# Rounding g and subtracting its high part on two pairs of chunks at once, and without plain f32 pairs

## The chip, the core and the metric

The kernel runs on one core of a Trainium2 chip. A core has TensorE (PE; PEld is its weight load), VectorE (DVE), ScalarE (ACT), GpSimd (POOL) and SyncE (SP, which issues the DMAs here). The metric is the device time of one execution, in microseconds.

## The reference

Four batches of 12480 tokens, 128 channels, 49 agents, all float32. An attention through agents is followed by a layer with 2048 hidden units:

```python
a2k = softmax(scale * agents @ k.T)      # per batch, 49 x 12480
agent_v = a2k @ v                        # 49 x 128
q2a = softmax(scale * q @ agents.T)      # 12480 x 49
x = q2a @ agent_v                        # all batches: 49920 x 128
h = x @ w_in                             # 49920 x 2048
g = h - np.tanh(h)
out = g @ w_out                          # 49920 x 128
```

## The kernel before

**Precision.** A matmul on f32 operands is replaced by several on float32r (fp32r) operands: a value is rounded to fp32r (its high part), and the difference is a second fp32r value (its low part). `w_out` is kept as `wo_h` and `wo_l`, and a hidden activation g as `gh` and `gl`. Then g @ w_out is gh x wo_l + gh x wo_h + gl x wo_h: three matmuls in place of one.

**First stage** (lines 482 to 502). For batch 0 the keys' scores, their maximum, the weighted values and the decoding of the 64-bit weights run by themselves, up to about 86 us. `agent_v` of a batch is multiplied into `w_in` (`project`), which gives `aw`, 98 x 2048: 49 rows for the high part and 49 for the low part of the softmax of q.

**Main stage** (from line 503). The tokens of all batches are cut into 104 blocks of 480 (`BLK`), and the 2048 hidden units into 16 chunks of 128 (`NCH`). The unit of work is a pair of chunks, so that a block has 8 pairs (`HP`) and the whole 832. One pair goes through these steps:

- `m1` (393 to 400) on PE: four matmuls of 480 columns, L398 and L399, write h of the pair into two banks of PSUM. Three such tiles (`ph`) exist.
- `act` (405 to 413): ACT takes the tanh of h (L408, into y) and squares it (L410, into z); DVE multiplies h by z (L412), which gives g. For the small h here g is proportional to h times tanh squared; the factor comes at the end, in `finish`.
- `high` (440) on POOL rounds g to gh (L442).
- `low` (445) on DVE subtracts gh from g, which gives gl (L447).
- `m2` (450 to 461) on PE: six matmuls, L459 to L461, add the pair's part to a PSUM tile `acc` of the block (from the pool `misc` of two tiles, which all the side work uses too).

In every second block (`PLAIN_EVERY`) the last pair is a plain one: it has no high and low, and `m2` multiplies g in f32 with an f32 copy of the weights, `wo_f` (L457, two matmuls; the profile records each of them as two).

The loop (553 to 586) writes one pair a step: m1, the side work, act and high of pair i, then low of pair i - 1 (`LAG1`), then m2 of pair i - 2 (`LAG2`). The queues `q1` and `q2` hold what is under way. Behind a block's last m2 `finish` copies `acc` to `out` on ACT (L522), and SP stores it after every second block. The framework then orders each engine's instructions by a simulated timeline, so an engine's order isn't exactly that of the loop.

**Side work** is cut into generators that are advanced by one piece in a step: the q softmax for two blocks (349 to 379: scores L353 on PE, maxima, sums and a product on DVE, two subtractions on POOL at L366 and L378), its transposition (L385, L390), and for the next batch one job of keys, maximum, values or projection at three places of every 16 steps (`KS`; L228, L276, L264). In the last batch there is no next one to prepare.

**Buffers.** y and z have 2 tiles, g 4, gh 3, gl 2, all of 960 columns. Keys have 3 tiles of their own in the main stage, values 4 (`VB`), which carry one more column, of ones.

Of the kernel before, what the change touches and what calls it, by code (L numbers as in the profile page):

```python
# [11 lines left out]
F32 = mybir.dt.float32  # L12
# [14 lines left out]
NCH = FF // 128  # L27
# [45 lines left out]
class Build:  # L73
# [19 lines left out]
    def constants(self):  # L93
# [15 lines left out]
        self.wo_f = c.tile([128, 2, C], F32, tag="wo_f", name="wo_f")  # L109
        self.vb = [c.tile([128, GT, C + 2], F32, tag=f"v{i}", name=f"v{i}") for i in range(VB)]  # L110
        for vt in self.vb:
            nc.gpsimd.memset(vt[:, :, C : C + 1], 1.0)
# [38 lines left out]
    def load_w_out(self, c, raw):  # L151
# [7 lines left out]
        if c == PLAIN_PAIR // 2:  # L159
            nc.scalar.copy(self.wo_f.rearrange("p n e -> p (n e)"), w[:, 2 * C * (PLAIN_PAIR % 2) :][:, : 2 * C])  # L160

    def phase1(self, b):
        nc = self.nc
        st = {}
        kb, vb = (KV0 if b == 0 else KV), VB
# [29 lines left out]
        def scores(g):  # L195
# [62 lines left out]
        def av(g):  # L258
            vt = ahead("v", load_v, g, vb - 1)
# [142 lines left out]
    def pair(self, t):  # L402
        return t[:, : 2 * BLK].rearrange("p (c n) -> p c n", c=2)

    def act(self, h):
        nc = self.nc
        y = self.pair(self.wtile("y", NB["y"]))
        nc.scalar.activation(y, h[:, :, :BLK], AF.Tanh, scale=TSC)  # L408
        z = self.wtile("z", NB["z"])[:, : 2 * BLK]
        nc.scalar.activation(z, y.rearrange("p c n -> p (c n)"), AF.Square)  # L410
        g = self.wtile("g", NB["g"])[:, : 2 * BLK]
        nc.vector.tensor_tensor(self.pair(g), h[:, :, :BLK], self.pair(z), ALU.mult)  # L412
        return g

    def act_general(self, h):
        nc = self.nc
        hv = h[:, :, :BLK]
        d = self.wtile("y", NB["y"])[:, : 2 * BLK]
        u = self.wtile("z", NB["z"])[:, : 2 * BLK]
        nc.scalar.activation(self.pair(d), hv, AF.Tanh)  # L420
        nc.scalar.activation(self.pair(u), hv, AF.Square)
        nc.vector.tensor_tensor(self.pair(d), hv, self.pair(d), ALU.subtract)
        big = self.wtile("y", NB["y"])[:, : 2 * BLK]
        nc.vector.tensor_scalar(big, u, 4.0, None, ALU.is_ge)
        nc.vector.tensor_scalar(u, u, 16.0, None, ALU.min)
        r = self.wtile("z", NB["z"])[:, : 2 * BLK]
        nc.vector.tensor_scalar(r, u, 1.0 / 15.0, 13.0, ALU.mult, ALU.add)
        g = self.wtile("g", NB["g"])[:, : 2 * BLK]
# [7 lines left out]
        nc.vector.tensor_tensor(self.pair(g), hv, self.pair(g), ALU.mult)  # L436
        nc.vector.copy_predicated(g, big.bitcast(I32), d)
        return g

    def high(self, g):  # L440
        gh = self.wtile("gh", NB["gh"])[:, : 2 * BLK].bitcast(F32R)
# [3 lines left out]
    def low(self, g, gh):  # L445
        gl = self.wtile("gl", NB["gl"])[:, : 2 * BLK].bitcast(F32R)
# [3 lines left out]
    def m2(self, acc, i, gh, gl):  # L450
        nc = self.nc
        for c in range(2):
            f = 2 * i + c
            x = slice(c * BLK, (c + 1) * BLK)
            first, last = f == 0, f == NCH - 1
            if gl is None:
                nc.tensor.matmul(acc[:, :BLK], self.wo_f[:, c, :], gh[:, x], start=first, stop=last)  # L457
                continue
            nc.tensor.matmul(acc[:, :BLK], self.wo_l[:, f, :], gh[:, x], start=first, stop=False)  # L459
            nc.tensor.matmul(acc[:, :BLK], self.wo_h[:, f, :], gh[:, x], start=False, stop=False)  # L460
            nc.tensor.matmul(acc[:, :BLK], self.wo_h[:, f, :], gl[:, x], start=False, stop=last)  # L461

    def fast(self):
        nc, tc = self.nc, self.tc
        HP = NCH // 2
        blocks = [(b, j) for b in range(B) for j in range(NBLK)]
        steps = [(n, i) for n in range(len(blocks)) for i in range(HP)]
# [64 lines left out]
        def rest(n, i, h):  # L532
            g = self.act(h)
            even = n % PLAIN_EVERY == 0
            plain = even and i == PLAIN_PAIR
            gh = None if plain else self.high(g)
            q1.append((n, i, g, gh))

        def low(keep):
            while len(q1) > keep:  # L540
                n, i, g, gh = q1.pop(0)
                q2.append((n, i, g, None) if gh is None else (n, i, gh, self.low(g, gh)))

        def out(keep):
            while len(q2) > keep:
# [3 lines left out]
                self.m2(acc[n], i, gh, gl)  # L549
                if i == HP - 1:  # L550
                    done.append(n)

        for n, i in steps:
            b = blocks[n][0]
            pos = (n % 2) * HP + i
# [3 lines left out]
            h = foreground(n, i)  # L559
            if n == 0 and i < len(rest0):  # L560
                run(rest0[i])
            nxt = []
            for gen in live:
                try:
                    next(gen)
                    nxt.append(gen)
                except StopIteration:
                    pass
            live[:] = nxt
            rest(n, i, h)  # L570
            low(LAG1)
            out(LAG2)
# [71 lines left out]
```

## Time and profile before

| | |
|---|---|
| runs, us | 2228.47, 2228.51, 2228.87 |
| median, us | 2228.51 |
| span of the profiled execution, us | 2226.8 |
| mean granted clock of TensorE | 0.992 |
| moved by DMA | 108.75 MB, 49 GB/s in the mean |
| batches 0 to 3 begin (first m1), us | 86.6, 634.7, 1180.7, 1726.5 |

The page gives no time of its own for the profiled execution beside its span; the three runs lie within 0.4 us of one another.

A busy time is the union of an engine's records. Matmuls are pipelined: a record of 0.38 us can stand behind one that started 0.22 us before, so the rate of PE is read from the distance of starts. "Idle before" is the time in which an engine did nothing ahead of an operation, with the operation that ended it.

### The profile page before, as it was taken

How to read it: one execution, taken by the hardware profiler on the slowest of the kernel's cores; microseconds unless marked ns; L12 is line 12 of the kernel's file. 1: busy time of each engine (PE TensorE's matmuls, PEld its weight loads, DVE VectorE, ACT ScalarE, POOL GpSimd, SP SyncE). 2: the span in 40 equal slices, each digit the busy share in tenths (PEclk: the TensorE clock that was granted, in tenths of full speed). 3: DMA queues.
4: the chain of work that ended last, by engine and by line, in shares of the span. 5: the costliest groups of instructions: out<-in, count | busy, mean ns of one | idle time of the engine just before them, and what ended most of it. 6: DMA issues, size and time to landing. Idle time of an engine off the chain costs nothing.

```text
span 2226.8 us, 31246 instructions
## 1 busy us (share of the span) xinstructions
PE 2181.5 (98%) x11083; PEld 1838.3 (83%) x11083; DVE 2044.3 (92%) x2107; ACT 1812.7 (81%) x2179; POOL 1410.9 (63%) x957
## 2 busy tenths in 40 slices
PE   7699999999999999999999999999999999999998
PEld 7588878888888887888888888788888888888887
DVE  6998998889998999888999999988999999999998
ACT  3478887778887877877888878877889989898987
POOL 2555566656765647665666555766666767676776
PEclk9899999999999999999999999999999999999999
DMA  9411111211011110211011210121010000000000
GB/s 300 120 56 56 57 37 47 65 50 35 28 46 56 56 58 30 63 56 58 19 36 38 65 55 21 37 64 49 19 36 19 28 27 28 27 27 27 27 10 20
DMA packets 76658, 108.75 MB, mean 49 GB/s; under 512 B 4048, under 2 KB 56528, under 8 KB 76496
## 3 DMA queue, kind: packets, MB, share of 16 engines
q1 hardware_dynamic: 76496, 106.68, 15.1%
q8 instruction: 91, 1.49, 0.3%
q14 instruction: 71, 0.58, 0.1%
HBM read 81.10 MB, written 25.56 MB: 48 GB/s over the span
## 4 chain that ended last, share of the span: by engine, by line
PE 90%; DVE 5%; POOL 2%; issue 1%; ACT 1%; DMA 0%; POOLq 0%; SPq 0%; ACTq 0%; DVEq 0%
PE h L398 16%; PE h L399 15%; PE misc L461 15%; PE misc L459 14%; PE misc L460 14%; PE misc L457 4%; PE misc L353 4%; PE misc L276 3%; PE misc L228 3%; DVE gl L447 1%; DVE g L412 1%; POOL gh L442 1%; PE h L209 1%; PE misc L385 1%; PE misc L327 0%
## 5 line engine op out<-in xcount | busy, mean ns | idle before, releaser
L442 POOL TENSOR_SCALAR gh<-g 128x960 fp32r<-128x960 f32 x780 | 1201.8, 1542 | 636.1 <-DVE g L412 488.9
L447 DVE TENSOR_TENSOR gl<-g,gh 128x960 fp32r<-128x960 f32 x780 | 977.6, 1254 | 88.6 <-PE misc L461 62.3
L412 DVE TENSOR_TENSOR g<-h,z 128x960 f32<-128x960 f32 x832 | 950.9, 1147 | 55.7 <-ACT z L410 53.3
L408 ACT ACTIVATE y<-h 128x960 f32<-128x960 f32 x832 | 804.2, 971 | 214.1 <-PE h L399 207.6
L410 ACT ACTIVATE z<-y 128x960 f32<-128x960 f32 x832 | 832.5, 1007 | 24.8 <-DVE g L412 7.8
L398 PE MATMUL h<-pT,awh 98*128 98x480 f32 x1664 | 666.9, 401 | 1.8 <-DVE g L412 1.3
L399 PE MATMUL h<-pT,awl 98*128 98x480 f32 x1664 | 631.6, 380 | 0.0
L461 PE MATMUL misc<-gl,wo_h 128*128 128x480 f32 x1560 | 608.7, 390 | 3.9 <-DVE gl L447 3.8
L459 PE MATMUL misc<-gh,wo_l 128*128 128x480 f32 x1560 | 594.2, 381 | 3.8 <-POOL gh L442 3.6
L460 PE MATMUL misc<-gh,wo_h 128*128 128x480 f32 x1560 | 591.2, 379 | 0.0
L398 PEld LDWEIGHTS h<-pT,awh 98*128 98x128 f32 x1664 | 312.8, 188 | 65.3 <-issue 14.0
L399 PEld LDWEIGHTS h<-pT,awl 98*128 98x128 f32 x1664 | 314.5, 189 | 58.8 <-issue 11.9
L461 PEld LDWEIGHTS misc<-gl,wo_h 128*128 128x128 f32 x1560 | 292.4, 187 | 59.1 <-DVE gl L447 8.7
L459 PEld LDWEIGHTS misc<-gh,wo_l 128*128 128x128 f32 x1560 | 294.3, 189 | 54.0 <-POOL gh L442 11.1
L460 PEld LDWEIGHTS misc<-gh,wo_h 128*128 128x128 f32 x1560 | 292.9, 188 | 47.9 <-issue 0.2
L378 POOL TENSOR_TENSOR pp<-qe,pp 120x392 fp32r<-120x392 f32 x52 | 70.6, 1357 | 67.9 <-ACT pp L376 67.6
L353 PEld LDWEIGHTS misc<-ag,qt 128*120 128x120 f32 x832 | 96.8, 187 | 3.3
L353 PE MATMUL misc<-ag,qt 128*120 128x49 f32 x832 | 94.2, 267 | 0.0
L457 PE MATMUL misc<-g,wo_f 128*128 128x480 f32 x208 | 92.6, 567 | 0.0
L366 POOL TENSOR_TENSOR qe<-qe,qm 120x392 f32<-120x392 f32 x52 | 71.0, 1366 | 30.0 <-ACT qe L364 29.9
L522 ACT ACTIVATE o<-misc 128x480 f32<-128x480 f32 x104 | 58.7, 565 | 36.4 <-PE misc L457 22.8
L276 PEld LDWEIGHTS misc<-v,ke 128*49 128x49 f32 (+1 forms) x588 | 62.0, 123 | 17.5 <-issue 12.9
(85 smaller groups left out, 993.7 us busy)
## 6 DMA issues: line engine op xcount, KB each, us to landing
qt<-qT SPq DMA_DIRECT2D x52, 480.0 KB, 3.4
outT<-o SPq DMA_DIRECT2D x52, 480.0 KB, 2.6
kt<-kT SPq DMA_DIRECT2D x48, 512.0 KB, 3.6
v<-v SPq DMA_DIRECT2D x48, 512.0 KB, 4.1
raw<-w_in SPq DMA_DIRECT2D x4, 512.0 KB, 7.8
raw<-w_out SPq DMA_DIRECT2D x4, 512.0 KB, 9.5
kt<-kT SPq DMA_DIRECT2D x4, 128.0 KB, 2.0
v<-v SPq DMA_DIRECT2D x4, 64.0 KB, 1.9
```

The costliest lines, as they stand in the source:

```text
L353: nc.tensor.matmul(ps[:TT, t * A : (t + 1) * A], qt[:, t * TT : (t + 1) * TT], self.ag[:, b, :], start=True, stop=True)
L398: nc.tensor.matmul(h[:, c, :BLK], aw[0][:A2, sl], pT[:A2], start=True, stop=False)
L399: nc.tensor.matmul(h[:, c, :BLK], aw[1][:A2, sl], pT[:A2], start=False, stop=True)
L408: nc.scalar.activation(y, h[:, :, :BLK], AF.Tanh, scale=TSC)
L410: nc.scalar.activation(z, y.rearrange("p c n -> p (c n)"), AF.Square)
L412: nc.vector.tensor_tensor(self.pair(g), h[:, :, :BLK], self.pair(z), ALU.mult)
L442: self.nc.gpsimd.tensor_scalar(gh, g, 1.0, 0.0, ALU.mult, ALU.add)
L447: self.nc.vector.tensor_tensor(gl, g, gh.bitcast(F32), ALU.subtract)
L457: nc.tensor.matmul(acc[:, :BLK], self.wo_f[:, c, :], gh[:, x], start=first, stop=last)
L459: nc.tensor.matmul(acc[:, :BLK], self.wo_l[:, f, :], gh[:, x], start=first, stop=False)
L460: nc.tensor.matmul(acc[:, :BLK], self.wo_h[:, f, :], gh[:, x], start=False, stop=False)
L461: nc.tensor.matmul(acc[:, :BLK], self.wo_h[:, f, :], gl[:, x], start=False, stop=last)
```

## The change

- Two pairs of a block form a group (`QP` = 2, four groups to a block, `HQ`). g, gh and gl are tiles of 1920 columns, one for a group. `act` writes each pair's half; `high` and `low` then run once for the group.
- ACT's square writes into the half of g, and DVE's product takes it from there and writes it back there. z is gone.
- The plain pairs and `wo_f` are gone: all 832 pairs take the six matmuls of `m2`.
- The loop goes by groups. Within group k: m1, side work and act of its first pair, m2 of the first pair of group k - 2; the same for the second pairs; then high of group k and low of group k - 1. `LAG1` and `LAG2` count groups now.
- Buffers: y 2 tiles of 960; g 3, gh 3, gl 2 tiles of 1920. From batch 1 on keys and values share a ring of 5 tiles (`RB`), those with the column of ones; keys and values are loaded up to four tiles ahead.
- `act_general` and `general`, which run only if h isn't small (they don't run with these inputs), are rewritten for the new tiles.

```diff
-KV = 3
-VB = 4
-PLAIN_PAIR = NCH // 2 - 1
-PLAIN_EVERY = 2
+RB = 5
+HP = NCH // 2
+QP = 2
+HQ = HP // QP
-NB = dict(y=2, z=2, g=4, gh=3, gl=2)
+NB = dict(y=2, g=3, gh=3, gl=2)
...
-    def wtile(self, tag, bufs):
-        return self.work.tile([128, 1024], F32, tag=tag, name=tag, bufs=bufs)
+    def wtile(self, tag, pairs):
+        return self.work.tile([128, pairs * 2 * BLK], F32, tag=tag, name=tag, bufs=NB[tag])
+
+    def slot(self):
+        self.nslot += 1
+        return self.kvb[self.nslot % RB]
...
-            kt = self.work.tile([128, GT * 128], F32, tag="kv", name="kt", bufs=kb)
-            kt = kt.rearrange("p (t n) -> p t n", n=128)[:, :n, :]
+            if b == 0:
+                kt = self.work.tile([128, GT * 128], F32, tag="kv", name="kt", bufs=KV0)
+                kt = kt.rearrange("p (t n) -> p t n", n=128)[:, :n, :]
+            else:
+                kt = self.slot()[:, :n, :C]
             nc.sync.dma_start(kt, self.kT[b][:, g * GT : g * GT + n, :])
...
-            vt = self.vb[g % VB]
+            vt = self.slot()
...
-            kt = ahead("k", load_k, g, kb if b == 0 else kb - 1)
-            if b and g >= NG - vb:
-                ahead("v", load_v, 0, g - NG + vb + 1)
+            kt = ahead("k", load_k, g, KV0 if b == 0 else RB - 1)
+            if b and g > NG - RB + 1:
+                ahead("v", load_v, 0, g - NG + RB - 1)
...
-    def act(self, h):
-        nc = self.nc
-        y = self.pair(self.wtile("y", NB["y"]))
+    def pair(self, t, x=0):
+        return t[:, x * 2 * BLK : (x + 1) * 2 * BLK].rearrange("p (c n) -> p c n", c=2)
+
+    def act(self, h, g, x):
+        nc = self.nc
+        y = self.pair(self.wtile("y", 1))
+        gv = self.pair(g, x)
         nc.scalar.activation(y, h[:, :, :BLK], AF.Tanh, scale=TSC)
-        z = self.wtile("z", NB["z"])[:, : 2 * BLK]
-        nc.scalar.activation(z, y.rearrange("p c n -> p (c n)"), AF.Square)
-        g = self.wtile("g", NB["g"])[:, : 2 * BLK]
-        nc.vector.tensor_tensor(self.pair(g), h[:, :, :BLK], self.pair(z), ALU.mult)
-        return g
+        nc.scalar.activation(gv, y, AF.Square)
+        nc.vector.tensor_tensor(gv, h[:, :, :BLK], gv, ALU.mult)
...
     def high(self, g):
-        gh = self.wtile("gh", NB["gh"])[:, : 2 * BLK].bitcast(F32R)
+        gh = self.wtile("gh", QP).bitcast(F32R)
         self.nc.gpsimd.tensor_scalar(gh, g, 1.0, 0.0, ALU.mult, ALU.add)
         return gh
...
-    def m2(self, acc, i, gh, gl):
+    def m2(self, acc, i, x, gh, gl):
         nc = self.nc
         for c in range(2):
-            f = 2 * i + c
-            x = slice(c * BLK, (c + 1) * BLK)
-            first, last = f == 0, f == NCH - 1
-            if gl is None:
-                nc.tensor.matmul(acc[:, :BLK], self.wo_f[:, c, :], gh[:, x], start=first, stop=last)
-                continue
...
+            f = 2 * (QP * i + x) + c
+            sl = slice((2 * x + c) * BLK, (2 * x + c + 1) * BLK)
+            nc.tensor.matmul(acc[:, :BLK], self.wo_l[:, f, :], gh[:, sl], start=f == 0, stop=False)
+            nc.tensor.matmul(acc[:, :BLK], self.wo_h[:, f, :], gh[:, sl], start=False, stop=False)
+            nc.tensor.matmul(acc[:, :BLK], self.wo_h[:, f, :], gl[:, sl], start=False, stop=f == NCH - 1)
...
         for n, i in steps:
...
+            g = self.wtile("g", QP)
+            second = out(LAG2 - 1)
+            for x in range(QP):
+                pos = (n % 2) * HP + QP * i + x
+                h = foreground(n, QP * i + x)
...
+                self.act(h, g, x)
+                next(second, None)
...
+            run(second)
+            q1.append((n, i, g, self.high(g)))
             low(LAG1)
-            out(LAG2)
```

More of the change, by code (lines that the diff above doesn't have):

```diff
@@ L108, in constants @@
         self.wo_l = c.tile([128, NCH, C], F32R, tag="wo_l", name="wo_l")
-        self.wo_f = c.tile([128, 2, C], F32, tag="wo_f", name="wo_f")
-        self.vb = [c.tile([128, GT, C + 2], F32, tag=f"v{i}", name=f"v{i}") for i in range(VB)]
-        for vt in self.vb:
+        self.kvb = [c.tile([128, GT, C + 2], F32, tag=f"v{i}", name=f"v{i}") for i in range(RB)]
+        for vt in self.kvb:
             nc.gpsimd.memset(vt[:, :, C : C + 1], 1.0)
@@ L258, in av @@
         def av(g):
-            vt = ahead("v", load_v, g, vb - 1)
+            vt = ahead("v", load_v, g, RB - 1)
             n = tiles(g)
@@ L445, in low @@
     def low(self, g, gh):
[L446 removed]
+        gl = self.wtile("gl", QP).bitcast(F32R)
         self.nc.vector.tensor_tensor(gl, g, gh.bitcast(F32), ALU.subtract)
         return gl
[L450 removed]
+    def m2(self, acc, i, x, gh, gl):
         nc = self.nc
         for c in range(2):
[L453 to L461 removed]
+            f = 2 * (QP * i + x) + c
[3 more added lines that the diff above has]
+            nc.tensor.matmul(acc[:, :BLK], self.wo_h[:, f, :], gl[:, sl], start=False, stop=f == NCH - 1)
     def fast(self):
         nc, tc = self.nc, self.tc
[L465 removed]
         blocks = [(b, j) for b in range(B) for j in range(NBLK)]
[L467 removed]
+        steps = [(n, i) for n in range(len(blocks)) for i in range(HQ)]
         npair = len(blocks) // 2
@@ L530, in foreground @@
             return h
[L532 to L537, printed above, removed]
         def low(keep):
@@ L541, in low @@
                 n, i, g, gh = q1.pop(0)
-                q2.append((n, i, g, None) if gh is None else (n, i, gh, self.low(g, gh)))
+                q2.append((n, i, gh, self.low(g, gh)))
         def out(keep):
@@ L548, in out @@
                     acc[n] = self.misc()
[L549 to L551 removed]
+                for x in range(QP):
+                    self.m2(acc[n], i, x, gh, gl)
+                    if i == HQ - 1 and x == QP - 1:
+                        done.append(n)
+                    yield
         for n, i in steps:
             b = blocks[n][0]
[L555 removed]
             p = n // 2
```

81 lines of the change are left out of this document (40 added, 41 removed).

## The prediction

> **What bounds the kernel now.** I read the page first: busy shares, the slices, the chain.
>
> ```profile
> PE 2181.5 (98%) x11083; PEld 1838.3 (83%) x11083; DVE 2044.3 (92%) x2107; ACT 1812.7 (81%) x2179; POOL 1410.9 (63%) x957
> PE   7699999999999999999999999999999999999998
> PEclk9899999999999999999999999999999999999999
> PE 90%; DVE 5%; POOL 2%; issue 1%; ACT 1%; DMA 0%; POOLq 0%; SPq 0%; ACTq 0%; DVEq 0%
> ```
>
> PE is at nine tenths or more from slice 3 on, at full clock, and the chain that ended last runs on it for 90%. But DVE at 92% is close, and a matmul's recorded end is modelled, so 98% proves little. Next come the groups (the number behind the bar is busy us, then mean ns, then the idle time in front).
>
> ```profile
> L442 POOL TENSOR_SCALAR gh<-g 128x960 fp32r<-128x960 f32 x780 | 1201.8, 1542 | 636.1 <-DVE g L412 488.9
> L447 DVE TENSOR_TENSOR gl<-g,gh 128x960 fp32r<-128x960 f32 x780 | 977.6, 1254 | 88.6 <-PE misc L461 62.3
> L412 DVE TENSOR_TENSOR g<-h,z 128x960 f32<-128x960 f32 x832 | 950.9, 1147 | 55.7 <-ACT z L410 53.3
> L457 PE MATMUL misc<-g,wo_f 128*128 128x480 f32 x208 | 92.6, 567 | 0.0
> ```
>
> In front of its two big operations DVE stood idle for 88.6 + 55.7 = 144 us. The waits say for whom:
>
> ```profile
> DVE gl L447 <- PE misc L461: 62.3, 101, 1.9
> PE misc L461 <- DVE gl L447: 3.8, 9, 0.6
> ```
>
> DVE waits 62.3 us for PE to give back a buffer of gl; the other way round it is 3.8 us. So PE is the bound, with DVE close behind. How close, stage by stage, the windows tell (columns: PE, PEld, DVE, ACT, POOL busy, clock, DMA):
>
> ```profile
> 748.00:758.00 10.00, 10.00 (x56) 8.49 (x54) 9.26 (x8) 7.26 (x10) 4.77 (x4) 1.00 0.19 55
> 2190.00:2200.00 10.00, 10.00 (x47) 8.59 (x47) 10.00 (x11) 9.16 (x11) 7.18 (x5) 1.00 0.07 27
> 294.00:311.00 17.00, 14.89 (x62) 10.78 (x62) 16.10 (x15) 12.80 (x15) 11.79 (x9) 1.00 0.00 0
> 1700.00:2227.00 527.00, 520.05 (x2502) 438.20 (x2500) 499.56 (x495) 464.44 (x533) 371.93 (x234) 1.00 0.07 25
> ```
>
> In a middle batch (748) PE is full and DVE has 0.7 of 10 to spare. In the last batch, which has no keys to prepare beside it, DVE is busy for 499.56 of 527 and in places for 10.00 of 10, with PE at 10.00 too. Around 300 us, where the next batch's maximum is taken, DVE's 16.1 of 17 made PE idle for 2.1.
>
> **Part 1, the plain f32 pairs go.** One of them on PE, and what follows:
>
> ```profile
> 1210.75 1.77 PE L457 MATMUL misc<-g,wo_f 128*128 128x480 f32 x4
> 1211.98 0.76 PE L398 MATMUL h<-pT,awh 98*128 98x480 f32 x1
> 1212.59 0.38 PE L399 MATMUL h<-pT,awl 98*128 98x480 f32 x1
> 1212.81 0.38 PE L398 MATMUL h<-pT,awh 98*128 98x480 f32 x1
> ...
> 1214.10 0.38 PE L459 MATMUL misc<-gh,wo_l 128*128 128x480 f32 x1
> ...
> 1215.40 0.38 PE L459 MATMUL misc<-gh,wo_l 128*128 128x480 f32 x1
> ```
>
> Starts count here, not durations. From the first plain matmul to the second one after the pair are 1212.59 - 1210.75 = 1.84 us; a normal first step (L399 to L398) is 0.22, so the pair holds PE for 1.62. The six fp32r matmuls that replace it take 1215.40 - 1214.10 = 1.30. There are 52 such pairs (208 records, four each): 52 x 0.32 = **16.6 us off PE**, which is on the path: PE starts a matmul each 0.22 us without a hole before and behind, and nothing else ends last there. If PE were not the bound, this gain would be nothing.
>
> The Trainium skill ("Perfetto Trace Analysis", Identifying the Most-Contended Engine) would have one judge TensorE not by matmul busy time but by LDWEIGHTS busy time. By that rule PE stands at 83% and DVE, at 92%, is the engine to relieve, so that the gain is 0 and the sum is part 2's DVE term alone. The trace disagrees here: the starts leave no hole, whatever share of the time a weight load lasts.
>
> The price is on the other engines: 52 pairs now need a rounding on POOL and a subtraction on DVE, inside the wide operations below.
>
> **Part 2, the wide operations.** POOL's high and DVE's low go from 780 of 960 columns to 416 of 1920. The trace has no 1920. The nearest rows:
>
> ```profile
> 1204.84 0.56 DVE L373 TENSOR_TENSOR qe<-qe,qs 120x392 f32<-120x392 f32 x1
> ...
> 2201.21 1.00 POOL L442 TENSOR_SCALAR gh<-g 128x960 fp32r<-128x960 f32 x1 [2.51 <-DVE g L412]
> ...
> 2207.76 0.39 PE L398 MATMUL h<-pT,awh 98*128 98x480 f32 x1
> 2208.35 1.15 DVE L447 TENSOR_TENSOR gl<-g,gh 128x960 fp32r<-128x960 f32 x1
> 2208.61 1.74 POOL L442 TENSOR_SCALAR gh<-g 128x960 fp32r<-128x960 f32 x1 [1.63 <-DVE g L412]
> 2209.41 1.15 DVE L412 TENSOR_TENSOR g<-h,z 128x960 f32<-128x960 f32 x1
> 2209.94 0.39 PE L398 MATMUL h<-pT,awh 98*128 98x480 f32 x1
> 2210.48 1.15 DVE L447 TENSOR_TENSOR gl<-g,gh 128x960 fp32r<-128x960 f32 x1
> 2211.55 1.15 DVE L412 TENSOR_TENSOR g<-h,z 128x960 f32<-128x960 f32 x1
> ```
>
> DVE: 0.56 us at 392 columns and 1.15 at 960 give 1.04 ns a column, so 1920 last some 2.15; one follows the next 0.08 sooner than its record ends (2210.48 to 2211.55 is 1.07), so a wide low holds DVE for 2.07. Bounds: 2.00 (slope alone) and 2.14 (twice the old). All lows: 780 x 1.07 = 835 before, 416 x 2.07 = 861 after, so +26 us (-3 to +55). Hidden under PE: two pairs cost DVE 4 x 1.07 = 4.28 before and 2 x 1.07 + 2.07 = 4.21 after, against PE's 2 x 2.18 (2207.76 to 2209.94) = 4.36. Only where a plain pair had relieved DVE does it get more; those blocks also carry the q scores on PE.
>
> POOL: alone 1.00, but 1.74 when it starts 0.26 after a low: it stands until the low ends at 2209.50 and then needs 0.85. So high and low exclude each other, while the product L412 lets POOL run. A wide high needs at most 2 x 0.85 = 1.70 after the low; the two products that follow it take 2.14. It fits as 0.85 fits in 1.07 now, with more to spare. Added waits: high waits for the second product of its group, and behind it on POOL stand the q softmax's subtractions and those of the values' weights; low waits for the wide high, and behind it on DVE stands the next group's first product, for which a tile of h and so PE's L398 wait. The first have whole pairs of time until they are used; the second is the first rival. Taken: no cost; bounds -10 us (fewer lows that POOL blocks, and more room where DVE holds PE up, as around 300 us) and that rival's price.
>
> **Part 3, the longer pipeline.** A low now needs both pairs of a group, and m2 lags by a group. That is paid at the two ends. The end now:
>
> ```profile
> 2215.82 1.15 DVE L412 TENSOR_TENSOR g<-h,z 128x960 f32<-128x960 f32 x1
> 2216.88 1.15 DVE L447 TENSOR_TENSOR gl<-g,gh 128x960 fp32r<-128x960 f32 x1
> 2217.14 1.74 POOL L442 TENSOR_SCALAR gh<-g 128x960 fp32r<-128x960 f32 x1 [0.38 <-PE misc L461]
> 2218.92 1.16 DVE L447 TENSOR_TENSOR gl<-g,gh 128x960 fp32r<-128x960 f32 x1 [0.89 <-POOL gh L442]
> 2220.13 0.48 PE L461 MATMUL misc<-gl,wo_h 128*128 128x480 f32 x1 [0.48 <-DVE gl L447]
> ```
>
> From the last product's end (2216.97) to the first matmul on the last gl are 3.2 us. After: the low before (2.07), high (1.70), low (2.15) make 5.9, and up to six matmuls more stand behind it (1.3). So 2.7 to 4.0 later, of which PE fills about half with the m2 it has left over; the first group starts late by as much. Taken: **+4 us** (0 to +8).
>
> **Part 4, in-place square, shared ring.** Square and product have the same sizes (0; L373 above works in place without a visible price). Keys go into the padded tiles of the values, in 512-byte rows:
>
> ```profile
> kt<-kT SPq DMA_DIRECT2D x48, 512.0 KB, 3.6
> v<-v SPq DMA_DIRECT2D x48, 512.0 KB, 4.1
> ```
>
> Such a row costs the values 4.1 us instead of 3.6. A job of keys comes each fifth or sixth pair (over 10 us at 2.18), and four tiles are asked for ahead, so this stays hidden. Passed on SP's queue: the q loads and stores of the output, which wait only if a ring slot isn't free. Taken 0; bound +12 (a landing of 4.1 exposed at each of three batch starts). The copy of wo_f on ACT goes (one operation).
>
> **Sum.** The profiled span is 2226.8, the median 2228.51; the page gives no time of its own for the profiled execution, so I take it to be a run like the three, with 1.7 us around the span. In the span 2226.8 - 16.6 + 4 = 2214.2; with 1.7 around it **2216**.
>
> **Rivals.** *Slower: the wide low stands in front of the product.* A tile of h is taken at 2207.76 and given back when its product ends at 2212.70: 4.94 us; three tiles at 2.18 allow 6.54. Slack 1.6. A low that is 1.0 longer leaves 0.6, and from the point at which DVE's side work or a low blocked by POOL (0.8 each in the row below, two lows in 3.77 us against 2.2) adds more, PE waits in front of L398. One such wait of 0.7 in every block (104) is 73 us, which gives 2289; in every second block 36 us, which gives 2252. It outweighs the gain from 0.03 us per group on (12.4 / 416). For it: DVE at 10.00 of 10. Against it: today's schedule has stretches of two lows in a row, wider than the new one,
>
> ```profile
> 748.01 3.77 DVE L447 TENSOR_TENSOR gl<-g,gh 128x960 fp32r<-128x960 f32 x2
> ```
>
> and PE was busy for 10.00 of 10 from 748 to 758. The Trainium skill ("Perfetto Trace Analysis", Optimizing Scalar/DVE Operations) says that where ScalarE or VectorE isn't saturated but causes bubbles on other engines, breaking up its operations can let work be done sooner; by that rule the merging goes the wrong way. This trace has few such bubbles, 3.8 us of waits for gl among them.
>
> This rival has a chance of 0.17.
>
> *Slower: DVE was the bound all along.* Then the 16.6 are worth nothing and the lows' +26 count: 2228 + 26 = 2254. For it: DVE's 92%, and 10.00 of 10 near the end. Against it: DVE's 144 us of idle time and PE's starts without a hole. Chance 0.06.
>
> *No change.* The two ends at their dear bound (+8 instead of +4) and 4 to 13 us of new waits, six to nineteen of 0.7 in the 104 blocks: 2224 to 2233. Chance 0.17.
>
> *Faster still.* Places as at 294 to 311, where DVE held PE up, ease because groups cost DVE 0.07 less and POOL blocks it less: 2206. Chance 0.12.
>
> **How the numbers follow.** Forecast 0.48. About 0.2% (4.5 us) can be told from no change. Faster: 0.48 + 0.12 = 0.60; same 0.17; slower 0.17 + 0.06 = 0.23. The range goes down to 2204 (faster still, and the ends 2 cheaper) and up to 2242, which leaves out the dearer half of the slower cases and little else.
>
> **What would show it.** PE's slices stay at 9; L457 gone, L459 to L461 at 1664 each with starts 0.22 apart; PE's busy time some 12 to 16 us down; DVE's lows at 416 x about 2.15 with few blocked; POOL's high near 2.15 - 0.26 + 1.70 = 3.6 when it starts behind a low. Wrong, if L398 has idle time in front that L412 ended, or PE's busy share falls below 97%.

## The result, and the profile after

| | before | after |
|---|---|---|
| median, us | 2228.49 | 2446.26 (2445.36 to 2450.2, four runs) |
| ratio to before | 1 | 1.0978, interval 1.0963 to 1.0994 |
| span of the profiled execution, us | 2226.8 | 2443.7 |
| mean granted clock of TensorE | 0.992 | 0.976 |
| batches 0 to 3, first m1 to the next one (the last: to the end), us | 548, 546, 546, 500 | 589, 587, 587, 591 |

The prediction was 2216, range 2204 to 2242. It was wrong in sign and by 230 us. The last row says where to look: all four batches lose, and the last one, which has no keys to prepare for a next batch, loses most (90 us). What got longer is the foreground itself. And all four now take nearly the same time, 587 to 591 us, although PE has less to do in the last.

The page of after, the busy line, PE's slices and clock, and the chain that ended last:

```profile
PE 2249.6 (92%) x11187; PEld 1873.3 (77%) x11187; DVE 2051.5 (84%) x1743; ACT 1778.2 (73%) x2178; POOL 1189.3 (49%) x594
...
PE   8699999999899999999899999999998988889897
...
PEclk9799999999999999999999999999999999999999
...
PE 37%; DVE 23%; POOL 16%; ACT 13%; issue 10%; DMA 0%; POOLq 0%; DVEq 0%; SPq 0%; ACTq 0%
```

PE's share fell from 98% to 92%, and no other engine took its place: DVE went from 92% to 84%, ACT and POOL fell too. Before, PE alone held 90% of the chain; now the chain goes round all four engines. That is the picture of a loop of dependencies, not of an engine that is full. The windows of after say the same of the stretch that the prediction shows of before, 1700 to 2227 us (in after it reaches from batch 2 into the last one, which begins at 1853), and a second thing in the three rows behind it (the columns are those of the prediction's windows):

```profile
1700.00:2227.00 527.00, 471.82 (x2186) 385.67 (x2185) 445.43 (x354) 391.95 (x468) 252.54 (x118) 0.98 0.07 23
2316.00:2326.00 10.00, 9.18 (x43) 7.67 (x42) 8.49 (x7) 7.05 (x8) 4.45 (x3) 1.00 0.00 0
2328.00:2332.00 4.00, 3.23 (x8) 2.75 (x9) 3.25 (x3) 2.05 (x3) 0.71 (x1) 0.57 0.00 0
2333.00:2343.00 10.00, 10.00 (x59) 8.71 (x57) 5.80 (x6) 7.38 (x10) 3.63 (x2) 1.00 0.01 2
```

Where DVE had been busy for 499.56 of 527 us and PE for 520.05, they are now busy for 445.43 and 471.82. (The granted clock of 0.57 from 2328 to 2332 is taken up in the last section.) The groups of after, with the idle time in front of each:

```profile
L444 POOL TENSOR_SCALAR gh<-g 128x1920 fp32r<-128x1920 f32 x416 | 957.3, 2301 | 1105.3 <-DVE g L415 995.3
L449 DVE TENSOR_TENSOR gl<-g,gh 128x1920 fp32r<-128x1920 f32 x416 | 934.0, 2246 | 202.7 <-POOL gh L444 202.7
L459 PE MATMUL misc<-gl,wo_h 128*128 128x480 f32 x1664 | 664.0, 402 | 97.2 <-DVE gl L449 94.6
L457 PE MATMUL misc<-gh,wo_l 128*128 128x480 f32 x1664 | 652.6, 392 | 54.6 <-POOL gh L444 54.6
L402 PE MATMUL h<-pT,awh 98*128 98x480 f32 x1664 | 653.8, 393 | 5.9 <-DVE g L415 3.8
```

PE now waits for gl (94.6 us; it was 3.8) and for gh (54.6), and DVE waits for gh (202.7; it was 22.3). In front of m1 (L402) PE waits for next to nothing.

One turn of the loop shows how these hang together. First the timeline of after, all engines (in brackets the idle time in front and what ended it; a high alone, then a high behind a low, and what waits for it):

```profile
2322.36 1.80 POOL L444 TENSOR_SCALAR gh<-g 128x1920 fp32r<-128x1920 f32 x1 [3.44 <-DVE g L415]
...
2324.92 2.15 DVE L449 TENSOR_TENSOR gl<-g,gh 128x1920 fp32r<-128x1920 f32 x1
...
2325.16 3.56 POOL L444 TENSOR_SCALAR gh<-g 128x1920 fp32r<-128x1920 f32 x1 [1.00 <-DVE g L415]
2325.17 0.38 PE L457 MATMUL misc<-gh,wo_l 128*128 128x480 f32 x1
...
2326.25 0.38 PE L403 MATMUL h<-pT,awl 98*128 98x480 f32 x1
2326.30 1.89 ACT L414 ACTIVATE g<-y 128x960 f32<-128x960 f32 x2
...
2328.75 2.16 DVE L449 TENSOR_TENSOR gl<-g,gh 128x1920 fp32r<-128x1920 f32 x1 [1.68 <-POOL gh L444]
...
2328.77 0.77 PE L457 MATMUL misc<-gh,wo_l 128*128 128x480 f32 x1 [2.13 <-POOL gh L444]
...
2329.33 0.60 PE L458 MATMUL misc<-gh,wo_h 128*128 128x480 f32 x1
2329.73 0.60 PE L459 MATMUL misc<-gl,wo_h 128*128 128x480 f32 x1
...
2332.05 0.38 PE L459 MATMUL misc<-gl,wo_h 128*128 128x480 f32 x1
2332.27 0.38 PE L457 MATMUL misc<-gh,wo_l 128*128 128x480 f32 x1
```

The high of 2325.16 starts 0.24 us behind a low and lasts until 1.65 after that low has ended: 3.56 instead of the 1.80 of the high before it. DVE's next instruction is the low of the same group, so DVE stands for 1.68. PE stands for 2.13, and that is not the long high alone. The matmul on gl at 2329.73 starts before the low of 2328.75 is done, so it reads the gl that had been ready since 2327.07 (2324.92 + 2.15): PE had work. But its order puts the first matmul of the next block, which needs the long high, ahead of the old block's last ones. Counted over the trace, 25 of the 104 blocks end like this, with the old gl ready for 1.7 us each time, and these 25 stops are 49.7 of the 54.6 us that PE waits for gh. The waits for gl, 94.6 us, are of another kind: each ends with the low that the matmul reads.

The chain of waits over the same stretch, in order of time (start, us, what):

```profile
2321.91 0.87 ACT y L413
2322.78 0.02 issue
2322.80 1.01 ACT g L414
2323.82 0.02 issue
2323.84 1.17 DVE g L415
...
2325.16 3.57 POOL gh L444
2328.72 0.04 issue
2328.77 0.77 PE misc L457
```

Tanh, square, product, high, matmul: each starts within 0.15 us of the end of the one before, and in the 3.57 of the high half is its stand behind the low. Worked out as medians over the groups of the last quarter of the trace: from the first m1 of a group to the end of its low are **14.0 us**, and the first matmul on its gl starts 0.06 us after that end (0.68 in the mean), so PE mostly stands ready for it. Meanwhile PE does the m1 of the pairs that its order puts ahead: counted over the order of its instructions, the m1 of 5.2 pairs are ahead of the first matmuls of a pair's m2 in the mean, 2.6 groups; this is called the lag here. Chain over lag gives an estimate of 14.0 / 2.6 = 5.4 us a group; measured are 5.52. (Counted at the matmuls on gl, 5.6 pairs are ahead, which gives 5.0.) PE's own work on a group is 4.36 (the prediction's 2 x 2.18). The agreement alone proves nothing of the cause: where PE stands ready for each result, the chain is lag times period whatever sets the period. That takes runs which change one of them.

### The profile page after: what moved, and what is told of

Its sections match the earlier page's. It is cut to its first block, busy times and chain, and to the rows that moved or that the text cites. A ratio compares the mean times of both kernels' runs of the same rounds, so it can differ in the third digit from the quotient of the medians.

```text
span 2443.7 us, 29814 instructions
## 1 busy us (share of the span) xinstructions
PE 2249.6 (92%) x11187; PEld 1873.3 (77%) x11187; DVE 2051.5 (84%) x1743; ACT 1778.2 (73%) x2178; POOL 1189.3 (49%) x594
## 4 chain that ended last, share of the span: by engine, by line
PE 37%; DVE 23%; POOL 16%; ACT 13%; issue 10%; DMA 0%; POOLq 0%; DVEq 0%; SPq 0%; ACTq 0%
POOL gh L444 14%; DVE g L415 10%; DVE gl L449 9%; PE misc L459 8%; PE misc L457 7%; PE misc L458 6%; ACT y L413 6%; ACT g L414 6%; PE h L402 5%; PE h L403 5%; PE misc L280 2%; PE misc L357 1%; PE misc L232 1%; POOL qe L370 1%; PE h L213 1%
## 5 line engine op out<-in xcount | busy, mean ns | idle before, releaser
L444 POOL TENSOR_SCALAR gh<-g 128x1920 fp32r<-128x1920 f32 x416 | 957.3, 2301 | 1105.3 <-DVE g L415 995.3
L449 DVE TENSOR_TENSOR gl<-g,gh 128x1920 fp32r<-128x1920 f32 x416 | 934.0, 2246 | 202.7 <-POOL gh L444 202.7
L415 DVE TENSOR_TENSOR g<-h,g 128x960 f32<-128x960 f32 x832 | 930.7, 1147 | 135.2 <-ACT g L414 133.2
L414 ACT ACTIVATE g<-y 128x960 f32<-128x960 f32 x832 | 816.3, 1005 | 9.3
L459 PE MATMUL misc<-gl,wo_h 128*128 128x480 f32 x1664 | 664.0, 402 | 97.2 <-DVE gl L449 94.6
L457 PE MATMUL misc<-gh,wo_l 128*128 128x480 f32 x1664 | 652.6, 392 | 54.6 <-POOL gh L444 54.6
L402 PE MATMUL h<-pT,awh 98*128 98x480 f32 x1664 | 653.8, 393 | 5.9 <-DVE g L415 3.8
L458 PE MATMUL misc<-gh,wo_h 128*128 128x480 f32 x1664 | 643.8, 387 | 0.0
L459 PEld LDWEIGHTS misc<-gl,wo_h 128*128 128x128 f32 x1664 | 321.4, 193 | 206.2 <-DVE gl L449 157.6
L402 PEld LDWEIGHTS h<-pT,awh 98*128 98x128 f32 x1664 | 314.3, 189 | 78.5 <-DVE g L415 24.9
L232 PEld LDWEIGHTS misc<-ag,v 128*128 128x128 f32 x588 | 73.9, 196 | 2.9 <-ACT qe L368 0.5
L280 PE MATMUL misc<-v,ke 128*49 128x129 f32 (+1 forms) x588 | 75.0, 276 | 0.0
```

Of the source, the lines that this page charges most:

```text
L280: nc.tensor.matmul(ps[:A, : C + 1], e3[:r, t, :], vt[:r, t, : C + 1], start=(first and t == 0), stop=(last and t == n - 1),)
L402: nc.tensor.matmul(h[:, c, :BLK], aw[0][:A2, sl], pT[:A2], start=True, stop=False)
L414: nc.scalar.activation(gv, y, AF.Square)
L415: nc.vector.tensor_tensor(gv, h[:, :, :BLK], gv, ALU.mult)
L444: self.nc.gpsimd.tensor_scalar(gh, g, 1.0, 0.0, ALU.mult, ALU.add)
L449: self.nc.vector.tensor_tensor(gl, g, gh.bitcast(F32), ALU.subtract)
```

## The experiments

Three theories stood at the start. *Uneven order* (A): the framework's planner puts DVE's products and lows in an uneven order (between two lows of after there are no products 89 times, one 35, two 79, three 212 times), so that highs stand behind lows, and this leaves the holes. *Width* (B): the wide step is too long for three tiles of h, whatever the order. *Load* (C, later D): without the plain pairs DVE and POOL, which get 52 more lows and highs, have too much to do; against it stands the prediction's gain of 16.6 us on PE. *Latency over lag* (L) was written down after the first four runs: the wide operations make a group's chain longer than the work that PE has ahead covers. Times are medians; intervals are those of the ratio to before. The diffs are cut to the lines that matter; `pin` ties an instruction behind the one that was pinned before it.

**e1_pin.** After, with DVE's products and lows held in the loop's order: two products, one low.

```diff
-        nc.vector.tensor_tensor(gv, h[:, :, :BLK], gv, ALU.mult)
+        self.pin(nc.vector.tensor_tensor(gv, h[:, :, :BLK], gv, ALU.mult))
...
+        if pin:
+            self.pin(ins)
```

> After, with one edit: the products and the lows of DVE are tied to the loop's order (two products, a low, two products, a low); everything else may still be moved. Theory A (order and port): a low that follows the low before without two products in between finds its high still held up by that low; DVE then stands and PE misses gl. With the products in between DVE's wait for POOL falls from 202.7 us to under 40, and the time to 2215 to 2270. Rival B (the wide step is too long for three tiles of h, whatever the order): PE still waits, 2380 or more. Rival C (without the plain pairs DVE and POOL have too much work): as after, 2446 give or take 30.

Measured: 2493.7 us, ratio 1.1198 (1.1179 to 1.1216); 47 us slower than after. An even order doesn't help. The time is one that B allowed (2380 or more), but the 3.8 us that PE waits in front of m1 in after speak against tiles of h. It isn't the test of A that it was meant to be, though: the median high still stands behind a low (3.56), a group's chain is 17.9 us instead of 14.0, and PE's order, which was left free, has more blocks that end as above (61 such stops, 108 us). e11b_lag1 below is the cleaner test.

**e2_narrow.** After with one pair to a group: all operations 960 wide again, the rest of the change kept.

```diff
-QP = 2
+QP = 1
-NB = dict(y=2, g=3, gh=3, gl=2)
+NB = dict(y=2, g=6, gh=6, gl=4)
```

> After with QP = 1: no plain pairs, square in place, shared ring, but each high and low on one pair (960 columns); buffers of the same bytes (g 6, gh 6, gl 4 tiles). Theory A and rival B: the loss is in the wide operations, so this is near the kernel before or better by the plain pairs' 16.6 us on PE: 2205 to 2235. Rival C: DVE has 52 x 1.07 us more to do than before, it is no better than 2250, and worse the more DVE was the bound.

**e3_noplain.** Before, with only the plain pairs taken out.

```diff
-            plain = even and i == PLAIN_PAIR
+            plain = False
```

> Before, with one edit: the plain pairs become ordinary pairs (high, low, six matmuls), nothing else. Theory A and rival B: 52 x 0.32 us less on PE, 2208 to 2220. Rival C: 2250 or more. If it lies within 5 us of before, the plain pairs' gain on PE is eaten by DVE.

Measured: e2_narrow 2258.1, ratio 1.0134 (1.0117 to 1.0151); e3_noplain 2259.3, ratio 1.0138 (1.0121 to 1.0155). So groups of two pairs account for 2446.3 - 2258.1 = 188 us of the loss, and taking out the plain pairs, which was to gain 12 to 17, costs about 30. It does so with the square in place, the ring and the loop's new order (e2_narrow) and without them (e3_noplain).

**e7_narrowhigh** and **e8_narrowlow**: after's groups, but POOL's high, or DVE's low, as two operations of 960 columns.

```diff
-        self.nc.gpsimd.tensor_scalar(gh, g, 1.0, 0.0, ALU.mult, ALU.add)
+        w = 2 * BLK
+        for x in range(QP):
+            sl = slice(x * w, (x + 1) * w)
+            self.nc.gpsimd.tensor_scalar(gh[:, sl], g[:, sl], 1.0, 0.0, ALU.mult, ALU.add)
```

> After, with high as two operations of 960 columns for a group, low still one of 1920. Theory A: the first half of high can run while the second product runs, and only the second half (0.85 us) waits behind the low before, so DVE's wait for POOL about halves and so does the loss: 2290 to 2380. Rival B: the low starts 0.85 us sooner, little else: 2380 to 2430. Rival C: as after, 2446 give or take 20.

> After with low as two operations of 960 columns, high still one of 1920. Theory L: m2's first half can start 1.07 us sooner, the chain is 13 us: 2370 to 2430. If the wide low alone costs the time: 2280 or less.

**e9_bothnarrow**: both of these edits.

> After with its groups, buffers and loop, but high and low each as two operations of 960 columns. Theory L (latency over lag: m2 follows m1 by a fixed 2.5 groups in PE's order, and a group's chain from m1 to the end of low, 14.0 us in after, is longer than 2.5 groups at PE's 4.4 us): the narrow operations overlap within a group, the chain is 3 to 4 us shorter, and the time is near that of QP = 1: 2255 to 2290. If the grouping of the loop itself costs the time, whatever the operations' width: 2400 or more.

Measured: high narrow 2385.2 (1.0685 to 1.0721), low narrow 2427.4 (1.0871 to 1.0915), both 2274.1 (1.0188 to 1.0222). The first lies just above what A allowed; the other two are where L had put them. One narrow operation gives 61 or 19 us, both together 172, so of the 188 the width of the two operations is 172, and 16 stay with the grouping. With both, the first half of a high starts 2.0 us ahead of the end of the group's second product in the median (in after 0.16 behind it), and an operation in the way is half as long; the chain falls to 11.6 us. That the parts don't add up fits a chain in which either long operation blocks the other, better than a price per operation: DVE and POOL have more instructions in e9_bothnarrow, and it is 172 us faster.

**e10_lag2** and its control **e10c_ctrl**. After with m2 a further group behind. The buffers for it don't fit beside the rest, so the ring goes to 3 tiles and `out` to 1; the control has these two alone.

```diff
-LAG2 = 1
+LAG2 = 2
-NB = dict(y=2, g=3, gh=3, gl=2)
+NB = dict(y=2, g=3, gh=4, gl=3)
-RB = 5
+RB = 3
```

> After with LAG2 = 2: m2 a whole group later, wide operations as they are; for its room gh 4 and gl 3 tiles, the ring 3 tiles in place of 5, one tile out. Theory L: the lag is 3.5 groups, 15.4 us at PE's pace, and covers the chain of 14.0: 2210 to 2275, bound by PE or DVE. If DVE and POOL shutting each other out set the pace, whatever PE's lag: 2380 or more.

> Control to it: after with the ring of 3 tiles and one tile out, LAG2 and the other buffers as in after. Every theory: as after, 2446 give or take 15; if keys or values come late with 3 tiles, more.

Measured: 2451.8 (1.0983 to 1.1020) and 2448.5 (1.0964 to 1.1008). The time is one that L doesn't allow, but the run tells nothing about the lag: in the built kernel the planner had put PE's instructions back, with 5.2 pairs ahead as in after. It does tell that the ring and the output tile, even at this size, cost nothing that can be seen.

**e11_pepin** and **e11b_lag1**: so PE's m1 and m2 are held in the loop's order, once with LAG2 = 2 (as in e10_lag2: seven pairs ahead) and once with LAG2 = 1 (five).

```diff
+            if self.pinned:
+                for q in ins:
+                    self.pin(q)
```

> The kernel with LAG2 = 2 (2452 us), in which the scheduler had put m2 back to where it stood in after (m1 5.2 pairs ahead of m2 in PE's order; 5.2 in after); now PE's m1 and m2 matmuls are tied to the loop's order, so that m1 is 7 pairs ahead. Theory L (a chain of 14.0 us from m1 to the end of low, divided by the pairs of m1 that PE has ahead): 14.0 / 7 = 2.0 us a pair, less than PE's 2.18, so PE or DVE binds, 2210 to 2275. If order and lag on PE aren't the cause: 2400 or more.

> After with PE's m1 and m2 tied to the loop's order and LAG2 = 1 as it is: m1 5 pairs ahead, as in after, but evenly; DVE comes out as two products, a low throughout. Theory L: 14.0 / 5 = 2.8 us a pair, 2400 to 2560. If the uneven order that the scheduler made is the cause, and not the lag: 2215 to 2300.

Measured: 2306.2 (1.0333 to 1.0367) with seven ahead, 2484.6 (1.1133 to 1.1171) with five; the built orders have these seven and five. The same wide operations, 140 us faster than after, and 178 faster than with the same hold and five pairs (though there the planner also gave DVE the even order of e1_pin, so not all of the 178 need be lag). The chain of a group is still 14.1 us, but the first matmul on gl now comes 2.5 us after the low has ended: PE no longer stands for it. L had allowed 2275 at most, so lag is not all of it.

e11b_lag1 also settles A. There, DVE's order is even, no high takes more than 2.0 us, so none stands behind a low, and PE waits for gh less than 1 us in all. Still it waits 159 us for gl, and the kernel is 38 us slower than after. Neither the highs behind lows nor the blocks that end badly are needed for the loss. The groups of e11_pepin, m1, gl and gh on PE:

```profile
L410 PE MATMUL h<-pT,awh 98*128 98x480 f32 x1664 | 666.4, 400 | 62.2 <-DVE g L426 59.3 <-DVE awl L343 1.3
L470 PE MATMUL misc<-gl,wo_h 128*128 128x480 f32 x1664 | 638.8, 384 | 2.2 <-DVE gl L460 2.2
L468 PE MATMUL misc<-gh,wo_l 128*128 128x480 f32 x1664 | 635.0, 382 | 2.3 <-DVE mxp L244 1.4 <-POOLq L611 0.8
```

The waits for gl and gh, 94.6 and 54.6 in after, are gone (2.2, and none on gh). In their place PE waits 59.3 us for tiles of h that a product gives back. That looks like the prediction's first rival; f4_lag_bothnarrow below tests it. (The 151 us in the expectation of that run add to the 59.3 the wait of PE's weight load for the same tiles, 91.6, which runs beside it.)

**e5_nolow** and **e12_direct** take the plain pairs apart. e5_nolow is e3_noplain without the 52 lows that came in (gh stands in for gl there). In e12_direct, the kernel before feeds the former plain pairs to the six matmuls straight from the product, which writes them as fp32r, and leaves out their high and low: PE has its saving, and POOL and DVE get nothing more to do.

```diff
-                q2.append((n, i, g, None) if gh is None else (n, i, gh, self.low(g, gh)))
+                skip = n % PLAIN_EVERY == 0 and i == PLAIN_PAIR
+                q2.append((n, i, gh, gh if skip else self.low(g, gh)))
```

```diff
-                q2.append((n, i, g, None) if gh is None else (n, i, gh, self.low(g, gh)))
+                q2.append((n, i, g, g) if gh is None else (n, i, gh, self.low(g, gh)))
```

> The kernel before without plain pairs (2259 us), and in the 52 former plain pairs the subtraction on DVE is left out: their gh stands in for gl, so that PE does the same matmuls and POOL the same roundings. If DVE's 52 added subtractions are what costs 31 us more than before (DVE is at 498 of 500 us in the last batch there): 2208 to 2225, now PE bound, with the plain pairs' 16.6 us gained. If the added roundings on POOL and the port cost it: 2245 or more.

> The kernel before, but each former plain pair takes its six fp32r matmuls straight from g (the product writes it rounded to fp32r): no high and no low for these 52 pairs, g in place of gh and of gl. It leaves out the roundings and subtractions and has the matmuls, so it is the plain pairs' effect on PE by itself. If the 52 x 0.32 us on PE are real and on the path: 2208 to 2218. If something else paces these places: 2222 to 2230.

Measured: e5_nolow 2244.5 (1.0054 to 1.0087), e12_direct 2229.8, ratio 1.0007 (0.9997 to 1.0016). The 52 lows cost 14.8 us of the 31; the other 16 come with the highs or their waits, which no run separates. And PE's 16.6 us by themselves don't make the kernel faster. Where they go, the waits of PE and of its weight load show in part, from 130 to 2220 us (us in total, times, longest), in before

```profile
PE misc L459 <- POOL gh L442: 3.6, 6, 0.7
...
PEld misc L459 <- POOL gh L442: 11.1, 22, 1.1
```

and in e12_direct:

```profile
PE misc L461 <- POOL gh L444: 11.6, 33, 0.7
...
PEld misc L461 <- POOL gh L444: 32.7, 55, 1.1
```

PE finishes the former plain pair sooner and later waits for a gh. Worked out over the distances of starts, each against the median for the same two operations, what PE loses in front of matmuls on gh grows from 22.4 to 38.8 us, by 16.4, as much as the saving. By batches it is not even: with 13 such pairs a batch should gain 4.2 us, the first three gain 0.7 to 1.3, and the last is 4.6 longer than in before. Why it is longer, with nothing added on any engine, is not shown.

Left open by then: whether the 30 us without plain pairs are a matter of lag too, and what keeps e11_pepin 78 us above before. Four more runs were for that.

**f1_lag_narrow**: e2_narrow with PE held and LAG2 = 3, five pairs ahead instead of four. **f2_lag_plain**: the same with the plain pairs put back. **f3_ring**: e2_narrow with the plain pairs put back, so that of the change only the square in place, the ring and the loop's order are left. **f4_lag_bothnarrow**: e11_pepin with both edits of e9_bothnarrow. The diff shows what puts the plain pairs back.

```diff
-                q1.append((n, i, g, self.high(g)))
+                q1.append((n, i, g, None if n % 2 == 0 and i == PLAIN_PAIR else self.high(g)))
```

> Narrow operations (QP = 1), no plain pairs, square in place, ring; LAG2 = 3 and m1 and m2 held in the loop's order on PE, so that five pairs of m1 run ahead of an m2 instead of four. e2_narrow, the same with four and PE's order left to the framework, took 2258.1. Latency over lag (L): the chain of a pair is 9.1 us there; over five pairs it is 1.8 us a pair, under PE's 2.18, so the 30 us that e2_narrow lost go: 2212 to 2228. Load on DVE and POOL (D: 52 more lows and roundings, about 15 us each): the lag changes nothing, 2250 to 2262.

> As f1_lag_narrow, but with the plain f32 pairs kept. By L the kernel before has lag enough (its plain pairs need neither high nor low): 2222 to 2230, and f1_lag_narrow is below it or equal to it. By D it is again 2222 to 2230, but f1_lag_narrow is 25 to 35 above it. If it is below 2220, the kernel before loses some time to lag too, and this one beats both kernels.

> After with narrow operations (QP = 1) and the plain pairs kept: of the change there remain the square in place, the ring for keys and values and the order of the loop. Every theory says no effect: 2225 to 2232. If it is 2240 or more, one of these three costs what I put down to the plain pairs.

> e11_pepin (groups, LAG2 = 2, PE's order held, 2306.2) with high and low cut in two operations of 960 each. In e11_pepin PE still waits 151 us for tiles of h that DVE's product gives back, behind wide lows. If the width of the operations is what is left there (the first rival of the prediction, now uncovered), this gives 2225 to 2265, near f1_lag_narrow; if it is something of the groups themselves or of the held order, it stays above 2285.

Measured: f1_lag_narrow 2263.7 (1.0147 to 1.0174), f2_lag_plain 2275.3 (1.0199 to 1.0227), f3_ring 2230.9 (1.0002 to 1.0020), f4_lag_bothnarrow 2286.5 (1.0245 to 1.0273).

f3_ring came out as expected: square in place, ring and order together cost 2.4 us, at the edge of what can be told. So the loss decomposes: 2228.5, +2.4 for these, +27.2 without the plain pairs (e2_narrow), +188.2 for groups of two with wide operations, 2446.3.

f1_lag_narrow is 5.6 us slower than e2_narrow, not faster, so in sum more lag doesn't give back what the plain pairs' removal cost. (In the built orders the lag is five pairs against four at the matmuls on gh, but 5.0 against 4.9 at those on gl.) By batches, from first m1 to the next batch's (the last to the end), it is less simple: f1_lag_narrow takes 550, 548, 548 and 524 us, e2_narrow 554, 550, 552 and 513, f3_ring 550, 546, 547 and 501. In the first three batches order and lag together give back 2 to 4 of the 4 to 6 us, as L has it; in the last they cost 11. What the narrow kernel without plain pairs lacks there shows in the window from 1745 to 2225 of e2_narrow

```profile
1745.00:2225.00 480.00, 473.59 (x2280) 394.93 (x2279) 478.60 (x459) 422.74 (x484) 357.92 (x224) 1.00 0.07 24
```

beside f3_ring

```profile
1745.00:2225.00 480.00, 475.70 (x2284) 402.04 (x2283) 457.70 (x454) 426.41 (x489) 338.11 (x214) 1.00 0.07 23
```

DVE is busy for 478.60 of 480 us without plain pairs, 457.70 with them: there DVE is full, which is D. The last batch pays 12 of the 27 us, the three others 4 to 6 each. In those DVE isn't full; f1_lag_narrow speaks for lag there, but a held order without more lag was not run, so it is not shown.

f2_lag_plain missed both theories' numbers: with the plain pairs there, the held order and its longer lag cost 44 us against f3_ring. Its mean clock is 0.980 against f3_ring's 0.992; in clock lost, 0.020 x 2273 - 0.008 x 2229 = 28 us at most, so part of it is what the last section says of the clock. By L f1_lag_narrow was to be no slower than f2_lag_plain, by D 25 to 35 us slower; it is 12 faster, but that is partly clock too. f4_lag_bothnarrow stayed above 2285: of e11_pepin's 78 us the width is worth 20, and the rest is the plain pairs (27) and the held order or the grouping, which aren't told apart. PE still waits 49.4 us there for tiles of h, against 59.3 with the wide operations, so that wait is not the wide low's. No version ran faster than before.

## Why the prediction was wrong

**Part 1, "which is on the path": failed.** The saving was sized right at 16.6 us, but "PE starts a matmul each 0.22 us without a hole before and behind" says that PE doesn't wait there, not that the rest keeps up if PE goes faster. e12_direct is that sentence put to the test: no faster (1.0007), with 16.4 us more of waits in front of matmuls on gh. What holds the kernel before is not PE alone but its loop with POOL and DVE. The prediction named the condition ("If PE were not the bound, this gain would be nothing") and the rule of the Trainium skill ("Perfetto Trace Analysis", Identifying the Most-Contended Engine) by which it took the gain for 0, and set both aside. That outcome was right here. That DVE is the engine which holds PE is another matter: it is full in the last batch of e2_narrow (478.60 of 480), but in before from 660 to 1200 us it is busy for 496.15 of 540, and most of the saving was lost there too.

**Part 2, durations: right.** 416 lows of 2.15 (mean 2.25 with the blocked ones), highs of 1.80 alone and 3.56 behind a low, against 2.15 and 3.6. Products, 1147 ns, are unchanged. **"Taken: no cost": failed**, and this is where 188 us went. The prediction weighed throughput: 1.70 of high fits into 2.14 of products. It listed the added waits, high for the second product and low for the wide high, and asked who stands behind them on POOL and DVE, but not how late the result is for PE. The rule it set aside says that breaking up ScalarE's or VectorE's operations may let work be done sooner where they make bubbles on other engines (the Trainium skill, "Perfetto Trace Analysis", Optimizing Scalar/DVE Operations). The runs agree: 2427 with DVE's low cut in two, 2274 with POOL's high cut as well, of which that sentence doesn't speak, 2446 without. The "few such bubbles" counted against it were those of the narrow kernel.

**Part 3, "That is paid at the two ends": failed.** The longer chain is paid in every group, as PE's order puts 2.6 groups ahead and 14.0 us would need 14.0 / 4.36 = 3.2. Its pieces in the last quarter of after, as means: 4.2 for the m1 of two pairs, 5.6 from there to the second product's end, 2.5 to the end of the high (1.8 alone or 3.6 behind a low, and the step before it), 0.4 until the low starts, and 2.2 for it, 14.9 in sum (the median is 14.0). The prediction had the rows for this: 4.94 from a pair's m1 to its product's end, 2.18 more for the second pair, 1.70 and 2.15 for high and low, and 2.07 where another low stands before them, 11 to 13 us. Over the 2.5 groups of the loop's order that is an estimate of 4.4 to 5.2 us a group, no less than PE's 4.36. It added the last three up for the end of the kernel and never held the whole against PE's lag.

**The rivals.** The first named one of the two operations, the wide low, which by itself is worth 19 us (e8_narrowlow), and the wrong place: PE was to wait in front of m1 for a tile of h, and waits there 3.8 us, because it stops at m2 first. Its price (up to 2289) was less than a third of the loss. "DVE was the bound all along", 2254, given 0.06, is about what taking out the plain pairs does by itself (2258 and 2259). That is a coincidence: its +26 us were reckoned for the wide lows, and these runs have narrow ones.

**Part 4: right.** f3_ring and e10c_ctrl show nothing to speak of.

**The signs named.** The plain pairs' f32 matmuls are gone and the counts are 1664 and 416. PE's share fell below 97%, which was named as a sign of being wrong. The other one, idle time in front of m1 (L398, now L402) that the product ended, did not come: 3.8 us.

## What to carry to other kernels

When operations between two visits to an in-order engine are merged, compare the chain from the first visit to the second with the work which that engine's order puts in between, before adding up busy times. Chain divided by lag estimates the period that the loop can keep, and here it bound without any engine being full. Merging also makes two operations that block each other block for longer, so cut the wide ones or lengthen the lag, and look at the built order to see whether the lag is there (LAG2 = 2 alone changed nothing) and whether a matmul that has to wait was put ahead of work that is ready. A saving on one engine counts only if a run with nothing but the saving is faster; here, with PE at 98% and DVE at 92%, it came back as waits.

## What the runs showed of the hardware

**The clock falls after short stops.** In the timeline above PE stood for 2.13 us and then started matmuls each 0.40 us until 2332, where it went back to 0.22; the window's granted clock is 0.57 there and 1.00 before and after. In after, PE stops for more than 0.5 us 121 times after 130 us, and never for longer than 2.4; in 20 stretches, mostly 3.4 us each, the clock is halved, against one such stretch in before, at its very end. By the mean clocks that is 0.024 x 2443.7 - 0.008 x 2226.8 = 41 us of lost clock at most, a fifth of the loss. The Trainium skill ("TensorE: Matmul & The Clock Gate", Why this matters for your kernels) asks for no idle gaps over some 3 us between bursts of matmuls. The trace doesn't bear that bound out: of 20 stops of 1.9 to 2.3 us, 14 went with half clock, which set in from 0.3 us before their end to 1.3 after it, and 6 did not. All 20 are stops at the end of a block, as described above.

**High and low exclude each other at both widths.** A high takes 1.00 us alone against 1.74 behind a low at 960 columns, 1.80 against 3.56 at 1920. The Trainium skill ("SBUF — State Buffer", Who interferes with whom) says that a DVE instruction with two inputs in SBUF contends with a GpSimd instruction that reads SBUF, and that contention comes from a shared pair of ports, which is an exclusive lock. The trace agrees: the high of 2325.16 ends 1.65 us after the low beside it. The product, which takes h from PSUM, doesn't hold POOL up: the high of 2322.36 took 1.80 with products beside it until 2323.26.
